# Reordering the opening of a two-layer attention kernel: exponentials of the gates behind copies of queries

## The chip, the cores and the metric

The kernel runs on one core of a Trainium2 chip. Its time is in device microseconds (us), from start to end of one execution; the span inside it runs from the first to the last profiled instruction. The engines are TensorE (PE, with its weight loads as PEld), VectorE (DVE), ScalarE (ACT), GpSimd (POOL) and SyncE (SP), which here only issues DMAs. Each engine works through its own queue in order and waits on semaphores for the others.

## The reference, cut to what matters

Two layers, each of an attention with a compressive memory (A) and a linear attention (B), over 2048 tokens of width 512 in 32 heads of 16.

```python
def _A_ref(x, wq, wk, wv, wo, beta):      # N = 4 segments of L = 512 tokens
    q, k, v = ...                         # x @ wq, x @ wk, x @ wv by head and segment
    phi = lambda t: jnp.where(t > 0, t + 1.0, jnp.exp(t))
    mask = (ar[:, None] < ar[None, :]) * -1e9
    g = sigmoid(beta).reshape(1, H, 1, 1) # one gate per head
    for s in range(N):
        p = softmax(qs @ ks.T * Dh ** -0.5 + mask)
        a_mem = (phi(qs) @ M) / (phi(qs) @ z + 1e-6)
        o = g * a_mem + (1.0 - g) * (p @ vs)
        M, z = M + phi(ks).T @ vs, z + phi(ks).sum()
    return o @ wo

x = A_x
for _ in range(2):
    x = x + _A_ref(layernorm(x), A_wq, A_wk, A_wv, A_wo, A_beta)
    x = x + _B_ref(layernorm(x), B_wqkv, B_w_phi, B_wo)
```

`_B_ref` projects to queries, keys and values, maps queries and keys through a small matrix per head and two softmaxes, and attends linearly.

## The kernel before, in words

The program is first written down as a list of 3416 numbered operations (`Program.add`), each with what it reads and writes and the engines that it may run on. Then `replay` deals them out by four tables that were written out beforehand: `ORDER` lists the operations in one sequence, from which every engine takes its own queue in that order (a number over 10000 is a matmul group that runs interleaved with the one before it, a negative one a filler of matmuls on zeros); `ENGINE` gives the engine of each operation that may run on several; `SLOTS` gives the buffer, or the bank of PSUM, of each tile when it is first used; and `AFTER` adds pairs (x, y) by which x waits for y although no data ask for it. `finalize` then writes every engine's queue with its semaphore waits.

```python
for n, x in enumerate(ORDER):
    if x < 0:
        f = self.idle_op((-1 - x) // 16, (-1 - x) % 16)
        ...
    op = ops[x % 10000]
    if len(op.eng) == 1:
        op.on = op.eng[0]
    op.need = set(op.deps)
    for t in list(op.pre) + op.tiles:
        if t.slot is None:
            k, p = int(next(slots), 36), t.pool
            ...                     # the tile waits for all users of the buffer's last holder
    self.queues[op.on].append(op.i)
for x, y in AFTER:
    ops[x].need.add(y)
```

The work is cut into segments of 512 tokens (for A) or chunks of 512 (for B) and tiles of 128 tokens. In the opening, `setup` loads four tiles of x, the weights of A and beta (`load`, L592; beta is the last of the six loads on ACT's queue), and then more loads on SP (`late_loads`), among them the raw key and query weights of B into two EQ buffers. `ln` normalizes the four tiles (statistics L806, L807; variance L816 and its power on POOL, L818; xn on DVE, L822) and TensorE transposes them (L606), with a copy to xA (L584). `a_proj` projects each tile: keys feature-major with three copies into K (L926 on ACT, L927 on DVE), scaled by the columns `even` 0 and 1 (L727), which keep one half of the heads; a shifted copy `lo` of xA (L912); a packed copy KP of K on POOL (L943); phi of the keys (exponential L834 on ACT, minimum L835 and sums L837 on DVE); queries with a copy into QT (L584); values with a copy into VT. The third and fourth tiles take their keys through `ktok` and a DMA transpose into K (L590).

The gates: exp(-beta) (L730) and exp(+beta) (L731) on ACT; from the second DVE makes the column `cb` = 1 + exp(beta) (L734), and copies it as the 17th column of each head into both VT buffers, four tiles each (L742, eight copies), so that the matmul of weights and values returns each head's sum divided by 1 - g. The first becomes g (L732, L733, L739), which scales the memory's state.

`a_att` computes scores in units of 1024 columns (L525), takes exponentials on ACT (L1109), masks the diagonal on DVE and POOL (L1115 with the pattern `modd`, L1118), multiplies by VT, divides (L1143, L1144) into O, and transposes O by DMA into OT for the output projection with WA_o. `fold_weights` turns the raw key and query weights of B, transposed by DMA from EQ into OT (four transposes, L590), into WB_k and WB_q.

Of the kernel before, what the change touches and what calls it, by code (L numbers as in the profile page):

```python
# [33 lines left out]
    0, 20, -401, 1, 2, 81, 4, 6, 8, 10, 3, 82, 5, 26, 7, 21, 24, 25, 9, 22, 11, 16, 53, 18, 54, 55, 60, 17, 56, 12, 61, 27, 62, 57, 63, 13, 35, 33,  # L34
    58, 64, 59, 67, 65, 84, 66, 68, 69, 85, 34, 74, 102, 70, 103, 86, 75, 104, 76, 71, 77, 115, 87, 105, 72, 83, 88, 89, 78, 106, 90, 73, 37, 91, 36,
    107, 116, 40, 45, 92, 96, 110, 46, 117, 47, 97, 38, 28, 48, 93, 29, 49, 157, 94, 98, 121, 50, 95, 30, 158, 209, 122, 346, 210, 123, 344, 31, 177,
    32, 347, 124, 133, 178, 212, 166, 10161, 345, 335, 125, 134, 348, 162, 349, 337, 79, 108, 51, 211, 127, 338, 426, 109, 336, 80, 167, 130, 128,
    339, 351, 340, 99, 350, 129, 131, 111, 352, 341, 118, 135, 342, 119, 168, 132, 112, 136, 343, 159, 1129, 179, 120, 214, 137, 160, 164, 163, 52,
    113, 138, 14, 169, 180, 100, 215, 114, 139, 145, 165, 146, 101, 1131, 140, 170, 182, 10193, 142, 143, 148, 181, 147, 183, 149, 144, 171, 172, 389,
    194, 173, 425, 187, 404, 126, 405, 150, 371, 185, 184, 174, 353, 188, 753, 198, 196, 406, 354, 746, 436, 199, 186, 355, 1138, 151, 195, 356, 200,  # L40
    15, 189, 1140, 197, 190, 359, 230, 152, 213, 380, 231, 191, 217, 232, 754, 192, 381, 755, 233, 201, 203, 368, 141, 216, 204, 382, 202, 175, 239,
    10234, 756, 744, 369, 240, 218, 176, 205, 206, 219, 220, 207, 235, 221, 222, 208, 757, 258, 223, 1141, 422, 224, 383, 39, 225, 263, 259, 43, 386,
    384, 1132, 370, 407, 387, 264, 423, 385, 427, 388, 242, 246, 10248, 438, 247, 424, 266, 362, 19, 260, 363, 236, 249, 439, 357, 153, 226, 758, 154,
    360, 364, 361, 244, 10250, 227, 365, 237, 228, 245, 446, 238, 372, 437, 229, 251, 241, 373, 252, 448, 243, 428, 374, 253, 1130, 447, 449, 366,
    268, 10270, 450, 375, 377, 429, 451, 254, 269, 367, 255, 440, -20, 453, 452, 271, 287, 378, 454, 261, 390, 256, 262, 1139, 288, 745, 430, 747,
    257, 272, 379, 1142, 441, 431, 282, 290, 273, 376, 391, 1143, 432, 392, 294, 283, 1133, 434, 433, 1134, 276, 393, 277, 395, 396, 289, 442, 435,
    295, 274, 1135, 464, 1136, 275, 465, 358, 1137, 1145, 475, 265, 291, 41, 467, 476, 443, 267, 466, 296, 10298, 42, 408, 297, 397, 278, 285, 284,
    279, 44, 299, 1144, 409, 280, 1146, 468, 483, 281, 477, 410, 292, 306, 478, 748, 398, 469, 411, 293, 286, 472, 470, 749, 473, 307, 414, 311, 474,
    479, 399, 413, 300, 312, 301, 308, 415, 316, 759, 302, 317, 760, 313, 320, 480, 416, 321, 750, 318, 751, 309, 417, 481, 319, 303, 400, 761, 310,
    322, 304, 484, 323, 1192, 314, 324, 315, 485, 752, 325, 482, 471, 571, 10566, 418, 326, 305, 567, 327, 1177, 412, 556, 328, 572, 329, 402, 330,  # L50
    587, 10582, 156, 155, 558, 401, 813, 574, 559, 419, 816, 831, 403, 583, 798, 394, 771, 569, 573, 772, 588, 420, 762, 814, 421, 557, 780, 562,
    10564, 590, 815, 773, 545, 565, 585, 561, 832, 331, 584, 546, 833, 547, 563, 586, 333, 332, 589, 774, 455, 619, 10614, 568, 777, 615, 334, 570,
    778, 456, 548, 457, 620, 575, 763, 549, 764, 591, 779, 603, 10641, 458, 765, 459, 550, 604, 592, 460, 593, 551, 795, 642, 461, 552, 462, 594, 595,
    622, 598, 463, 553, 768, 617, 646, 599, 616, 554, 618, 576, 577, 555, 766, 796, 647, 578, 600, 444, 621, 579, 797, 623, 445, 637, 639, 601, 638,
    1162, 624, 580, 625, 605, 626, 606, 486, 602, 581, 640, 487, 596, 775, 607, 597, 627, 608, 489, 628, 651, 769, 653, 776, 488, 609, 610, 770, 611,
    654, 807, 629, 490, 612, 497, 613, 652, 498, 631, 494, 630, 808, 500, 649, 632, 644, 499, 657, 10655, 491, 495, 658, 643, 505, 809, 506, 656, 492,
    645, 665, 811, 781, 501, 496, 666, 782, 659, 783, 660, 648, 502, 810, 670, 10679, 784, 650, 635, 503, 786, 493, 507, 680, 668, 633, 671, 636, 675,
    661, 812, 676, 662, 504, 836, 677, 667, 789, 678, 634, 785, 790, 834, 508, 669, 791, 663, 835, 837, 694, 10689, 787, 792, 838, 664, 510, 839, 509,
    695, 683, 672, 511, 684, 690, 840, 681, 841, 799, 788, 682, 842, 703, 673, 800, 674, 704, 699, 10701, 697, 801, 685, 700, 686, 793, 1147, 802,
    794, 512, 692, 687, 702, 825, 688, 691, 826, 513, 805, 804, 729, 10727, 693, 817, 728, 806, 696, 852, 818, 730, 698, 705, 819, 853, 706, 707, 820,  # L60
    823, 767, 708, 827, 855, 718, 10713, 854, 829, 709, 560, 710, 714, 856, 1163, 711, 1164, 712, 719, 863, 716, 857, 864, 822, 715, 1165, 723, 10725,
    1148, 724, 858, 717, 1149, 824, 860, 726, 720, 861, 721, 1150, 722, 731, 828, 862, 949, 10947, 1151, 803, 732, 948, 733, 734, 830, 950, 941, 735,
    736, 1159, 866, 942, 983, 10972, 865, 737, 930, 738, 984, 1168, 867, 931, 739, 871, 932, 973, 1160, 985, 1169, 868, 1166, 1161, 859, 951, 10988,
    821, 869, 1170, 872, 986, 975, 952, 1153, 873, 933, 974, 1154, 989, 742, 934, 976, 1155, 991, 990, 967, 10956, 743, 1171, 937, 740, 987, 968, 938,
    992, 845, 1178, 957, 1179, 969, 741, 935, 970, 846, 1180, 999, 843, 1004, 1000, 939, 1181, 971, 936, 1174, 1175, 844, 1172, 1005, 847, 977, 1173,
    978, 848, 993, 940, 994, 995, 1156, 979, 980, 850, 1026, 11042, 1176, 849, 996, 1157, 1198, 1027, 851, 1001, 1158, 1199, 1002, 997, 1189, 1043,
    953, 1007, 959, 1190, 1003, 1200, 998, 1024, 981, 1183, 1006, 1025, 982, 1184, 954, 958, 1008, 1009, 1201, 1010, 1185, 1022, 11031, 960, 874,
    1191, 1032, 875, 955, 1011, 1012, 876, 1034, 961, 962, 1013, 963, 877, 1014, 964, 870, 1033, 1023, 1040, 965, 878, 885, 966, 886, 1016, 1041, 882,
    1015, 888, 1028, 1036, 11038, 1017, 879, 887, 1204, 1167, 1037, 1205, 880, 889, 883, 1206, 1039, 1055, 11050, 1029, 893, 1187, 1030, 890, 1051,
    894, 1035, 1044, 891, 1045, 1056, 884, 1064, 1046, 1065, 1062, 1053, 1052, 895, 1047, 1020, 1063, 1048, 1186, 1049, 1066, 11060, 1021, 1018, 1054,  # L70
# [13 lines left out]
    1525, 923, 928, 1442, 1416, 1454, 1526, 1407, 1271, 1417, 1527, 1270, 1455, 1528, 924, 1418, 1459, 1426, 1272, 1287, 1428, 1460, 1529, 1288, 1433,  # L84
# [80 lines left out]
    3324, 3325, 3328, 3326, 3329, 3342, 3330, 3321, 3338, 3289, 3343, 3331, 3344, 3317, 3339, 3345, 3340, 3341, 3318, 3306, 3319, 3377, 3346, 3353,  # L165
    3378, 3380, 3354, 3355, 3356, 3357, 3381, 3335, 3358, 3359, 3360, 3387, 3336, 3361, 3383, 3388, 3389, 3332, 3390, 3384, 3385, 3337, 3386, 3307,
    3347, 3391, 3407, 3348, 3350, 3408, 3349, 3379, 3322, 3409, 3410, 3382, 3398, 3351, 3365, 3399, 3400, 3401, 3362, 3366, 3411, 3363, 3402, 3395,
    3333, 3364, 3412, 3403, 3334, 3392, 3396, 3404, 3393, 3413, 3394, 3405, 3367, 3397, 3414, 3406, 3352, 3415,
)
AFTER = (  # L170
    (21, 20), (23, 1246), (25, 82), (26, 82), (27, 60), (31, 346), (56, 55), (63, 60), (70, 34), (77, 76), (83, 67), (91, 78), (179, 112), (201, 754),
    (202, 141), (211, 345), (212, 346), (218, 216), (237, 361), (238, 227), (242, 385), (243, 227), (262, 378), (267, 1136), (286, 284), (289, 392),
    (290, 745), (291, 1145), (309, 750), (313, 415), (315, 1192), (339, 335), (340, 336), (349, 344), (407, 384), (450, 449), (451, 366), (468, 1144),
    (535, 1540), (570, 421), (574, 412), (575, 557), (584, 412), (589, 762), (590, 328), (602, 605), (617, 461), (645, 809), (648, 643), (667, 504),
# [1306 lines left out]
```

## Time and profile before

| | |
|---|---|
| Median of 3 runs | 470.28 us (469.51 to 471.39) |
| Profiled execution | 469.92 us |
| Its span | 468.2 us |
| Mean granted TensorE clock | 0.993 of full |
| Busy in the span: PE, DVE, ACT, POOL | 97%, 89%, 91%, 54% |
| Chain that ended last, by engine | PE 50%, ACT 33%, DVE 9%, DMA 3%, POOL 3% |

A row of the timeline gives start, length, engine, line, operation, what is written and read, and in brackets the idle time of the engine before it with what ended it. A row of the chain gives start, length and the engine with its tile. Rows of stretches give, for each engine, the busy time and the number of instructions, and then the clock that TensorE was granted. Ends of matmuls are modelled.

### The profile page before, as it was taken

To read this page: it belongs to the slowest core of one execution; us is meant where nothing else is said; L and a number is where in the kernel's file an instruction comes from. 1 tells how busy PE (TensorE), PEld (TensorE's weight loads), DVE (VectorE), ACT (ScalarE), POOL (GpSimd) and SP (SyncE) were. 2 spreads that over 40 slices of the span, in tenths; PEclk is the share of its full clock that TensorE was granted. 3 is DMA by queue.
4 is the path that set the end of the run, shared out by engine and by line. 5 is a ranking of instruction groups with operands and counts; after the bars stand their busy time and mean duration, and the time that the engine had idled before them with its cause. 6 is when DMAs were issued, how large, how long until landed. Compare 5 with 4: busy or idle time off the path is not lost.

```text
span 468.2 us, 18975 instructions
## 1 busy us (share of the span) xinstructions
PE 452.7 (97%) x8208; PEld 312.7 (67%) x8208; DVE 418.9 (89%) x1038; ACT 428.0 (91%) x665; POOL 251.0 (54%) x406
## 2 busy tenths in 40 slices
PE   7899999999999999999999999999999999999897
PEld 6686667677756556647778667777775756755653
DVE  6899999979998989788998999999999798988884
ACT  4899999999999999986999899999999999999633
POOL 3666646666755767520066372875686676741100
PEclk9899999999999989999999999999999999999999
DMA  8979742243211224120334346234341122631366
GB/s 266 199 172 170 104 71 48 48 70 69 48 26 26 48 46 64 31 57 14 69 76 86 70 63 100 48 70 76 67 67 25 25 47 50 92 48 24 69 132 183
DMA packets 115091, 35.85 MB, mean 77 GB/s; under 512 B 106816, under 2 KB 115008, under 8 KB 115008
## 3 DMA queue, kind: packets, MB, share of 16 engines
q1 hardware_dynamic: 112896, 32.80, 38.4%
q10 hardware_dynamic: 2112, 1.84, 1.2%
q8 instruction: 64, 1.05, 1.0%
q14 instruction: 19, 0.16, 0.1%
HBM read 6.32 MB, written 2.10 MB: 18 GB/s over the span
## 4 chain that ended last, share of the span: by engine, by line
PE 50%; ACT 33%; DVE 9%; DMA 3%; POOL 3%; issue 1%; ACTq 0%; POOLq 0%
PE PS L525 49%; ACT PT L1109 23%; ACT Ek L1205 3%; DMA beta<-in_A_beta_dram 2%; ACT EQ L1290 2%; POOL PT L1118 1%; DVE xn L822 1%; DVE Vt L1233 1%; DMA OT<-O 1%; POOL D L1115 1%; ACT QT L584 1%; ACT PT L1290 1%; ACT phi L964 1%; PE PS L606 1%; DVE D L1115 1%
## 5 line engine op out<-in xcount | busy, mean ns | idle before, releaser
L1109 ACT ACTIVATE PT<-PS 128x1024 bf16<-128x1024 f32 x288 | 282.0, 1062 | 5.8 <-PE PS L525 4.3
L1115 POOL TENSOR_TENSOR D<-PT,modd 128x256 bf16<-128x256 bf16 x118 | 80.7, 695 | 48.8 <-ACT PT L1109 21.1
L1118 POOL TENSOR_SCALAR_AFFINE_SELECT PT<-PT 128x512 bf16<-128x512 bf16 x128 | 82.6, 657 | 36.3 <-DVE D L1115 28.1
L525 PEld LDWEIGHTS PS<-VT,PT 128*128 128x128 bf16 x2048 | 74.4, 96 | 16.1 <-POOL PT L1118 1.9
L525 PE MATMUL PS<-VT,PT 128*128 128x17 bf16 x2048 | 81.0, 171 | 1.1 <-DVE O L1144 0.5
L525 PE MATMUL PS<-QT,K 32*128 32x64 bf16 (+2 forms) x2176 | 76.0, 214 | 2.4 <-ACT QT L584 1.7
L525 PE MATMUL PS<-VT,D 128*128 128x17 bf16 x512 | 59.5, 171 | 0.0
L525 PEld LDWEIGHTS PS<-QT,K 32*128 32x128 bf16 x2176 | 40.9, 93 | 20.3 <-ACT PT L1109 9.9
L1309 POOL COPY O<-rho 128x512 bf16<-128x512 bf16 x26 | 16.5, 656 | 52.0 <-DVE rho L1302 26.2
L525 PEld LDWEIGHTS PS<-VT,D 128*128 128x128 bf16 x512 | 43.2, 96 | 0.0
L1115 DVE TENSOR_TENSOR D<-PT,modd 128x256 bf16<-128x256 bf16 x138 | 40.4, 311 | 2.9 <-ACT PT L1109 1.6
L1212 POOL TENSOR_TENSOR Vt<-Ek 128x512 f32<-128x512 bf16 x24 | 28.0, 1167 | 24.1 <-ACT Ek L1205 18.9
L1233 DVE TENSOR_TENSOR Vt<-PS,Zk 128x1024 bf16<-128x1024 f32 (+1 forms) x34 | 38.9, 1154 | 0.4 <-PE PS L525 0.2
L806 DVE BATCH_NORM_STATS2 stats<-X 128x6 f32<-128x512 bf16 x56 | 37.5, 683 | 1.8 <-DMA X<-in_A_x_dram 1.4
L1205 ACT ACTIVATE Ek<-PS 128x512 bf16<-128x512 f32 x64 | 37.1, 653 | 1.8 <-PE PS L525 1.5
L1170 DVE TENSOR_TENSOR X<-X,PS 128x512 bf16<-128x512 bf16 x50 | 33.6, 680 | 3.2 <-PE PS L525 2.8
L525 PE MATMUL PS<-xA,WA_q 128*128 128x128 bf16 x512 | 36.0, 219 | 0.0
L525 PE MATMUL PS<-WA_k,xA 128*128 128x256 bf16 x256 | 35.7, 278 | 0.2
L525 PE MATMUL PS<-WA_v,xA 128*128 128x256 bf16 x256 | 35.5, 274 | 0.0
L525 PEld LDWEIGHTS PS<-xA,WA_q 128*128 128x128 bf16 x512 | 30.0, 98 | 4.4 <-issue 1.1
L525 PE MATMUL PS<-WB_o,OT 128*128 128x512 bf16 x128 | 32.2, 380 | 0.2 <-DMA OT<-O 0.2
L525 PE MATMUL PS<-WA_o,OT 128*128 128x512 bf16 x128 | 32.0, 380 | 0.4 <-DVE OT L584 0.2
(156 smaller groups left out, 938.7 us busy)
## 6 DMA issues: line engine op xcount, KB each, us to landing
X<-in_A_x_dram SPq DMA_DIRECT2D x3, 512.0 KB, 11.5
out_dram<-X SPq DMA_DIRECT2D x10, 128.0 KB, 1.9
EQ<-in_B_wqkv_dram SPq DMA_DIRECT2D x2, 512.0 KB, 5.6
out_dram<-X ACTq DMA_DIRECT2D x6, 128.0 KB, 2.4
OT<-O SPq DMA_TRANSPOSE x42, 3.2
WB_v<-in_B_wqkv_dram SPq DMA_DIRECT2D x1, 512.0 KB, 10.6
WA_o<-in_A_wo_dram SPq DMA_DIRECT2D x1, 512.0 KB, 3.9
WB_o<-in_B_wo_dram SPq DMA_DIRECT2D x1, 512.0 KB, 5.4
```

The lines of the kernel that those rows point to most:

```text
L525: return e.matmul(o, l, r, start=st, stop=sp, tile_position=(basep(l), basep(o)))
L584: emit = {"act": lambda e: e.activation(dst(), src(), ACT.Copy), "dve": lambda e: e.tensor_copy(dst(), src())}
L806: self.dve(lambda e, t=t, src=src: e.bn_stats(self.stats[:, t, :], src()), 0.603, [held() if held else R("X", t)], [R("stats", t)], name=" ...
L1109: self.act(lambda e, st=st, pt=pt: e.activation(pt.ap[:].rearrange("p b c -> p (b c)"), self.ps[:, st.slot[0] * 512:st.slot[0] * 512 + 102 ...
L1115: self.either(lambda e, d=d, k=k, pt=pt: e.tensor_tensor(d.ap[:, :, k, :].rearrange("p b (z c) -> p b z c", z=2), self.ends(pt.ap[:, :, 25 ...
L1118: self.pool(lambda e, q=quarters: e.affine_select(q(), q(), [[0, 4], [1, 128]], ALU.is_ge, 0.0, base=0, channel_multiplier=-1), 0.6, [pt() ...
L1170: self.dve(lambda e: e.tensor_tensor(X[:, t, :], X[:, t, :], self.bank(gen), ALU.add), 0.6, [R("X", t), gen()], [R("X", t)], name="resid")
L1205: self.act(lambda e, sgn=sgn, Ek=Ek, gen=gen: e.activation(Ek.ap[:, sgn, :], self.bank(gen), ACT.Exp, scale=1.0 - 2.0 * sgn), 512, [gen()] ...
L1212: self.pool(lambda e, Ek=Ek, sums=sums: e.tensor_tensor(sums(), *(Ek.ap[:].rearrange("p s (h j) -> p s h j", h=H)[:, :, :, 8 * k:8 * k + 8 ...
L1233: self.dve(lambda e, w=w, n=n, Vt=Vt, Zk=Zk, gen2=gen2: e.tensor_tensor(self.signed(Vt)[:, w, :, 0:16], self.bank(gen2).rearrange("p (h d) ...
L1290: self.act(lambda e, sgn=sgn, g=g, gen=gen: e.activation(E(sgn, g), self.bank(gen), ACT.Exp, scale=1.0 - 2.0 * sgn), 512, [gen()], [part(s ...
L1309: P.add(("act", "pool"), {"act": lambda e, dst=dst, src=src: e.activation(dst(), src(), ACT.Copy), "pool": lambda e, dst=dst, src=src: e.t ...
```

## The change

Only the four tables change. No operation is added or taken away. The first rows of `ORDER`, before and after:

```diff
 ORDER = (
-    0, 20, -401, 1, 2, 81, 4, 6, 8, 10, 3, 82, 5, 26, 7, 21, 24, 25, 9, 22, 11, 16, 53, 18, 54, 55, 60, 17, 56, 12, 61, 27, 62, 57, 63, 13, 35, 33,
-    58, 64, 59, 67, 65, 84, 66, 68, 69, 85, 34, 74, 102, 70, 103, 86, 75, 104, 76, 71, 77, 115, 87, 105, 72, 83, 88, 89, 78, 106, 90, 73, 37, 91, 36,
-    107, 116, 40, 45, 92, 96, 110, 46, 117, 47, 97, 38, 28, 48, 93, 29, 49, 157, 94, 98, 121, 50, 95, 30, 158, 209, 122, 346, 210, 123, 344, 31, 177,
...
+    22, 20, -401, 0, 1, 26, 81, 27, 3, 2, 82, 5, 4, 7, 6, 9, 8, 11, 10, 53, 16, 18, 54, 55, 60, 56, 17, 21, 61, 24, 62, 57, 25, 63, 58, 33, 59, 28,
+    64, 12, 67, 65, 84, 66, 74, 85, 68, 103, 75, 69, 86, 70, 104, 83, 102, 89, 71, 29, 90, 34, 76, 87, 105, 30, 115, 77, 88, 72, 106, 116, 92, 91, 73,
+    96, 107, 121, 97, 78, 110, 37, 117, 40, 45, 31, 98, 93, 46, 36, 47, 177, 94, 157, 346, 178, 209, 122, 95, 210, 48, 344, 123, 133, 49, 124, 32,
...
 AFTER = (
-    (21, 20), (23, 1246), (25, 82), (26, 82), (27, 60), (31, 346), (56, 55), (63, 60), (70, 34), (77, 76), (83, 67), (91, 78), (179, 112), (201, 754),
+    (23, 1246), (24, 60), (25, 62), (28, 33), (29, 74), (32, 344), (70, 75), (83, 68), (91, 71), (179, 112), (201, 754), (202, 141), (211, 344),
...
```

Read as queues of the engines, this is what changes:

| Engine | Order before | Order after |
|---|---|---|
| ACT | `lo` of tile 2; K copies 1a, 1b, 1c, 2b; exp(+beta); exp(-beta); K copy 2c; phi's exponential, tile 1; copies of queries, tiles 2 and 1; score exponentials 158, 210, 178 | K copies 1b, 1c; phi's exponential, tile 1; K copy 2c; exp(+beta); copies of queries, tiles 2 and 1; exp(-beta); score exponentials 178, 210, 158 |
| DVE | H8b, `even` 0, xn 2, statistics 3, `even` 1, statistics 4, xn 3, K copy 2a, xn 4, copy of xA 3, `cb`, VT columns among phi and statistics | `even` 0, xn 2, statistics 3 and 4, K copy 1a, `lo` of tile 2, xn 3, `even` 1, K copies 2a and 2b, copy of xA 3, `lo` of tile 3, xn 4, `cb`, VT columns, most of them later; H8b far later |
| PE | ... second tile's keys; queries 2 (first half); transpose 3; first tile's keys by head; queries 2, 1; scores 157, 209; third tile's keys; scores 177 | ... second tile's keys; first tile's keys by head; queries 2 (first half); transpose 3; queries 2, 1; scores 177, 157, 209; third tile's keys |
| POOL | `ident` and H8, power 1, ..., powers, `lo` 1, KP 1, KP 2, pieces of `modd`, `lo` 3 | `ident`, power 1, H8, power 2, pieces of `modd` among powers, `lo` 1, KP 1, KP 2 |
| SP | raw keys' load; transpose of K (tile 3); transpose of raw keys, first half; two transposes of xn; raw queries' load; transpose of K (tile 4); transpose of raw queries, first half; WA_o's load | transpose of K (tile 3); two transposes of xn; transpose of K (tile 4); raw keys' load; raw queries' load; transpose of raw queries, first half; transpose of raw keys, first half; WA_o's load |

(1a is the copy into K of the first tile that uses `even` 0; b and c are the two with `even` 1.) Behind the first 26 groups of PE, the first 27 of ACT, 22 of POOL and 18 of SP, and behind the first 68 of DVE (in the new count) save for H8b's cast, the queues are the same as before. The copies 1a and 2b and the `lo` copies of tiles 2 and 3 change engine (from ACT, ACT, ACT and POOL to DVE) in `ENGINE`. `SLOTS` deals the ten PT buffers and some others out in another rotation, so that tiles take turns with other tiles than before; the numbers of buffers are the same.

More of the change, by code (lines that the diff above doesn't have):

```diff
@@ L198 @@
 SLOTS = (
-    "10000204510210000310282090141131530052001212101030211400221133071110002302225001411216020123123210011117003511002829051043010104022504312005"
-    "40121090015402200014832234701023002543000421312501300315701034111200110511000381902011022111421110514052300005231703000216001110300102031112"
-    "20119081112100227003120303023002140120510112130716022140010200113012201211334315061203012100021317010351403133121311000332270611200340010200"
-    "00210050811313020191102301203120310202100914010301132001400308205022132253360232020150712112111601090224432805131123233701632509300322151221"
-    "04083034100302261932300230433113110010300240532035720201480526110011240003300022111322370222152410133042133410000809210320221511013201016031"
-    "00020403110021920010070222381010150311110042025376970010318250161123123103410220000413003223064331053203210302101007006722170135301620127261"
+    "00211311215020403010020704304105010022100401113180231023136051101000231122390114122101013211232300612115003911002428051043000107032504312005"
+    "60721080150402300114432234001020002553600421312007312035901030111300110511400301702011032110421300514022300005251903000218061110300103031112"
+    "21117001112100229005110303023003140120210112130419022180610210115012201311332318091203014130021316010021503133121811000332260910201320510220"
+    "00210040113313020131002301207180310202100512000301132301400107205022832253340932021100612112141501070224832905132143230601032507300322151241"
+    "08093034000302221732300230133113411010350240536035820201400922110011210003350022411326380222152410133002133410000107210320221419013221015031"
+    "00020003110061820010070222311010140391110022025375870010314210161123123103410220000413003223064331053203210302101007006722170135301620127261"
     "20175012102006401331317302020010827007621101600600523117002020280933204131003051101001070031211100120030226190321100041283113023102101302023"
@@ L210 @@
     "02133290151002102601350072073251252200021821403100112233000121511171101289640150346030120030010434112112151003521700211002210320322020312311"
-    "0233020076122306111204500160763027341"
+    "0233020076223106111204500160763027341"
 )
```

2 lines of the change are left out of this document (1 added, 1 removed), and 114 rows, old and new, of tables (AFTER, ORDER).

## The prediction

> **What bounds the kernel now.** I read the page's head, then the chain of work that ended last in the first 60 us, the timeline of the opening, the busy time by stretch, and the DMA issues with their landings.
>
> ```profile
> span 468.2 us, 18975 instructions
> PE 452.7 (97%) x8208; PEld 312.7 (67%) x8208; DVE 418.9 (89%) x1038; ACT 428.0 (91%) x665; POOL 251.0 (54%) x406
> ```
>
> Three engines are nearly full over the span. No engine's order changes past the opening but for one small cast, so only the opening can move. The chain there (start, length, what):
>
> ```profile
> 3.27 8.73 DMA beta<-in_A_beta_dram
> 12.00 0.02 issue
> 12.03 0.23 ACT rd L731
> 12.25 0.12 ACT rd L730
> 12.37 0.36 ACT K L926
> 12.73 0.49 ACT phi L834
> 13.22 0.98 ACT QT L584 x2
> ```
>
> Beta lands at 12.00. Between it and the two copies of queries stand two exponentials, a copy into K and an exponential of keys; the copies end at 14.20 and the score units follow. The idle gaps around it (in brackets, with what ended them):
>
> ```profile
> 10.56 1.50 PE L525 MATMUL PS<-xA,WA_q 128*128 128x128 bf16 x24
> 12.03 0.23 ACT L731 ACTIVATE rd<-beta 128x32 f32<-128x32 bf16 x1 [1.54 <-DMA beta<-in_A_beta_dram]
> 12.29 0.18 DVE L734 TENSOR_SCALAR cb<-rd 128x32 bf16<-128x32 f32 x1 [1.66 <-ACT rd L731]
> 13.76 0.39 PE L525 MATMUL PS<-QT,K 32*128 32x128 bf16 x8 [1.70 <-ACT QT L584]
> 16.71 0.69 DVE L584 CAST ktok<-PS 128x512 bf16<-128x512 f32 x1 [0.49 <-PE PS L525]
> 17.26 2.17 ACT L1109 ACTIVATE PT<-PS 128x1024 bf16<-128x1024 f32 x2 [1.12 <-PE PS L525]
> 19.13 0.42 DVE L584 COPY xA<-PS 128x512 bf16<-128x512 bf16 x1 [0.18 <-PE PS L606]
> ```
>
> ACT, DVE and PE each lose over 1.5 us around beta; after that only small gaps are left. By stretch (length; busy time and count of PE, PEld, DVE, ACT, POOL; granted clock; DMA share; GB/s):
>
> ```profile
> 4.00:7.41 3.41, 2.06 (x25) 1.57 (x23) 2.94 (x11) 1.84 (x3) 1.52 (x3) 1.00 1.07 362
> 10.83:14.24 3.41, 1.63 (x31) 1.29 (x28) 1.84 (x9) 2.21 (x7) 1.51 (x5) 1.00 1.12 363
> 14.24:17.65 3.41, 3.40 (x39) 2.22 (x40) 2.92 (x9) 2.29 (x3) 2.00 (x6) 0.50 0.68 205
> 20.00:30.00 10.00, 10.00 (x193) 8.89 (x191) 10.00 (x29) 10.00 (x16) 6.20 (x10) 1.00 1.06 170
> ```
>
> TensorE's clock was halved from 14.24 to 17.65, right after a stretch in which it was busy 1.63 of 3.41 us. From 20 to 30 PE, DVE and ACT are all full: what the opening saves reaches the end only as far as the slowest of the three passes it on.
>
> **The change, part by part.**
>
> *ACT.* Its order becomes: two copies into K of the first tile (both need the second `even` column), the key exponential, one more copy into K, exp(+beta), the two query copies, exp(-beta), the score exponentials. So only exp(-beta) goes behind the queries; exp(+beta) still waits until 12.00 in front of them. Two copies into K and a `lo` copy leave ACT for DVE. There the second `even` slides behind more work:
>
> ```profile
> 7.82 0.15 DVE L727 TENSOR_REDUCE even<-H 128x1 f32<-128x4 f32 x1
> 7.88 0.68 DVE L806 BATCH_NORM_STATS2 stats<-X 128x6 f32<-128x512 bf16 x1
> 8.33 2.15 ACT L926 ACTIVATE K<-PS,even 128x512 bf16<-128x512 f32 x4
> 8.60 0.18 DVE L807 BATCH_NORM_AGGREGATE mv<-stats 128x2 f32<-128x6 f32 x1
> 8.90 0.41 DVE L822 TENSOR_SCALAR xn<-X,mv,rstd 128x512 bf16<-128x512 bf16 x1
> 9.23 0.74 DVE L927 TENSOR_SCALAR K<-PS,even 128x512 bf16<-128x512 f32 x1
> 14.08 0.41 DVE L837 SCALAR_TENSOR_TENSOR PhiK<-PS,phi 128x256 bf16<-128x256 f32 x1
> 21.70 0.22 DVE L912 COPY xA<-xA 128x256 bf16<-128x256 bf16 x1
> ```
>
> 7.82 plus 0.68 and 0.18 (statistics), 0.74 (a K copy moved here), 0.22 (`lo`) and 0.41 (xn) puts it at 10.05, and about 9.95 since neighbours overlap a little. ACT then needs some 0.5 + 0.5 (four K copies took 2.15), 0.49 and 0.36 (the chain's rows), 1.85 us: done at about 11.9, which the wait for beta covers with 0.1 to spare; without that cover each us late is a us on the queries. The query copies start behind one exponential, at about 12.2 instead of 13.22, and end at 13.25 instead of 14.20: of the chain's terms 0.12, 0.36 and 0.49 go, 0.97 us.
>
> *PE.* The first tile's two key groups move ahead of the queries; the second waits for its `lo` copy. I put the end of the queries at 12.4 (12.06 now), still ahead of their copies. Then a score unit that needs both copies goes first, at about 13.30, where today the first unit starts at 13.76 and waits again for the second copy until 14.20. The score exponentials start at 13.75 instead of 14.20, 0.45 us; three units then stand in a row, so ACT's 1.12 gap goes too. ACT could gain 0.45 + 1.12 = 1.57.
>
> *The clock.* PE's idle in the stretch 10.83 to 14.24 shrinks from 1.78 to about 0.9 us, busy 74%, above the 60% (2.06 of 3.41) after which the clock stayed whole. I take it as whole. The price, from rows:
>
> ```profile
> 14.79 1.89 PE L525 MATMUL PS<-WA_k,xA 128*128 128x256 bf16 x8
> 22.66 1.05 PE L525 MATMUL PS<-WA_k,xA 128*128 128x256 bf16 x8
> ```
>
> 0.84 us for these eight alone, an estimated 1.4 for the 3.41 us. With the earlier start PE could gain up to 0.9 + 1.4 = 2.3. [...]
>
> *DVE.* Added before 12.29: the two K copies (0.74, and near 0.41 for the half-size one) and two `lo` copies (0.22 each), 1.59 us. Its idle 1.66 covers them, and H8b's cast leaves that stretch. The gate column `cb` still waits for exp(+beta), so the next work begins at 12.29 as now, and from there on it is the same work in another order: DVE can save only its gaps, 0.49 + 0.18 = 0.67.
>
> ```profile
> L742 DVE COPY VT<-cb x8: 220/242/705, 12.5 to 22.6; 128x32 bf16<-128x32 bf16 x8
> 26.19 0.23 PE L525 MATMUL PS<-VT,PT 128*128 128x17 bf16 x3
> ```
>
> VT's eight columns (median 0.24) slide back among DVE's work. Their reader stands at 26.19 and the last column now ends at 23.3: 2.9 us of cover, and 0.24 a column if that were gone.
>
> *New waits.* A key group on PE now needs a phi buffer that DVE frees at about 15.1, against 14.7 when PE could take it: 0.4 of PE idle, with the other key, value and score groups queued behind it. The first tile's values wait, as now, for DVE's xA copy (19.13), which gets more DVE work ahead: up to 1 us of PE idle. Both take from PE's 2.3, not from what it has today. POOL gets the mask's pieces and the powers in another order; busy for 54% of the span, it has room.
>
> *Buffers.* The ten PT buffers, and a few others, are dealt out in another rotation through the whole kernel, so a score unit waits for other earlier readers. By the trace's times each of these had ended when its buffer is taken again, give or take 0.07, so I put nothing. What PE waits for PT in all, over the span, is this row of its waits:
>
> ```profile
> PE PS L525 <- ACT PT L1109: 0.2, 1, 0.2
> ```
>
> Were such a wait to come up in each half of the kernel, it would cost some tenths.
>
> *SP.* The raw keys' load moves behind four transposes, next to the raw queries' load; behind those comes the raw queries' transpose, which holds SP until they land.
>
> ```profile
> 18.82 1.33 SPq L590 DMA_TRANSPOSE OT<-EQ  x1
> 24.03 0.58 SPq L592 DMA_DIRECT2D EQ<-in_B_wqkv_dram  x1
> 28.39 1.86 SPq L590 DMA_TRANSPOSE OT<-EQ  x1
> 35.55 1.23 SPq L590 DMA_TRANSPOSE OT<-O  x1
> EQ<-in_B_wqkv_dram SPq DMA_DIRECT2D x1, 512.0 KB, 6.8
> EQ<-in_B_wqkv_dram SPq DMA_DIRECT2D x1, 512.0 KB, 4.3
> 39.04 0.38 PE L525 MATMUL PS<-WA_o,OT 128*128 128x512 bf16 x1
> ```
>
> The raw queries would be issued near 26.4 (24.03 now) and land 4.3 to 6.8 later, 30.7 to 33.2. Behind them stand 1.86 + 1.33 + 0.58 = 3.77 of issues, so SP is free for the first attention output's transpose between 34.5 and 37.0. That output would be ready near 34.85 (35.55 less the gain). I take the lower end, no cost, since 4.3 was measured in this part of the kernel and 6.8 in the crowd of first loads.
>
> *Sum.* ACT 1.57, PE at most 2.3, DVE 0.67, and SP from 0 to a loss of 1.45 (35.55 to 37.0) at the bottom. I take 0.7, DVE's, because from 20 to 30 DVE is as full as the others and hands them their inputs. The profiled execution took 469.92 us (span 468.2 and 1.7 around it): 469.92 - 0.7 = 469.2. It stands 0.36 below the median of the three runs, so in medians 470.28 - 0.7 = **469.6 us**.
>
> **Rivals.**
> 1. *DVE does not hold it back.* What PE and ACT need goes first on DVE, VT's columns and the gate's arithmetic go last; ACT's whole 1.57 passes: 470.28 - 1.6 = 468.7. For it: DVE is 89% busy over the span and can catch up later. Against: the full stretch from 20 to 30.
> 2. *Slower: SP is late.* If the raw queries land 6.8 us after their issue, the output's transpose is issued at 37.0 instead of 35.55. PE takes its result in order at 39.04, 3.5 after the present issue, so it resumes at 40.5 at the latest and, with some slack, 1.2 later than today; everything queued on PE waits with it: 470.28 + 1.2 = 471.5. It begins to cost when they land past 31.1 (34.85 - 3.77) and turns the change into a loss past about 32. For it: two loads of 512 KB back to back behind a transpose. [...]
> 3. *It does not do what it says.* The second `even` comes 0.5 late or more, the copies of queries move little, the clock still halves: 0.2 is left, 470.1. For it: ACT's margin of 0.1 before 12.00. Against: DVE's 1.66 of idle for the extra work.
>
> **How the numbers follow.** Forecast 0.52; rival 1 0.22; rival 2 0.15; rival 3 0.11. Half a per cent is 2.35 us, about what a measurement of this kernel can tell from no change. No case reaches it alone; with the runs' scatter (469.51 to 471.39) part of rival 1 ends below 467.9 and part of rival 2 above 472.6: faster 0.10, same 0.82, slower 0.08. The range runs from rival 1 less 0.7 of scatter to rival 2: 468.0 to 471.5.
>
> **What would show it.** First score matmul near 13.3; PE's gap before it under 1.1; clock 1.00 from 14 to 18; no gap of ACT near 17; `cb` still at 12.3 and DVE full from there to 30 without the 0.49 and 0.18; the first output's transpose issued before 35.0. It is wrong if PE waits at the first output projection, if the half clock is still there, or if the span moves by more than 2 us either way.

## The result, and the profile after

| | Kernel before | Changed kernel |
|---|---|---|
| Median | 470.36 us (469.51 to 471.39, 4 runs) | 474.59 us (474.16 to 475.48, 4 runs) |
| Profiled execution, its span | 469.92, 468.2 | 474.83, 473.1 |
| Mean granted TensorE clock there | 0.993 | 0.993 |

The ratio is 1.0091, with a 95% interval of 1.0066 to 1.0117: slower by 4.2 us, where a gain of 0.7 was forecast. A second measurement (below) gave 1.0068 (1.0039 to 1.0098). The medians here and below are over all executions, the ratios leave out those in a disturbed state, among them the first profile of experiment 4, at a mean clock of 0.555.

Of the changed kernel, first the chain of work that ended last (start, length, what):

```profile
36.76 0.68 DVE VT L584 x2
37.44 4.72 DMA OT<-O
42.16 0.05 issue
42.21 7.28 PE PS L525 x64
```

A DMA now stands in it: the transpose of the first attention output, on which the first output projection waits. The timeline of SP's issues, and of TensorE at that place:

```profile
25.76 1.17 SPq L592 DMA_DIRECT2D EQ<-in_B_wqkv_dram  x2
33.08 3.69 SPq L590 DMA_TRANSPOSE OT<-EQ  x2
36.81 0.58 SPq L592 DMA_DIRECT2D WA_o<-in_A_wo_dram  x1
37.44 1.26 SPq L590 DMA_TRANSPOSE OT<-O  x1
...
38.36 0.40 PE L525 MATMUL PS<-VT,PhiK 128*128 128x136 bf16 x4
42.21 1.04 PE L525 MATMUL PS<-WA_o,OT 128*128 128x512 bf16 x2 [3.45 <-DMA OT<-O]
```

SP issues the two raw loads at 25.76 and then nothing until 33.08: its next entry, the transpose of the raw queries, waits for their landing at 33.06. WA_o's load and the output's transpose come behind both raw transposes. The output's transpose goes out at 37.44 (35.55 before), and TensorE resumes at 42.21 (39.04 before) after 3.45 us without work. Its DMA rows in that stretch (median us to landing last):

```profile
EQ<-in_B_wqkv_dram SPq DMA_DIRECT2D x2, 512.0 KB, 6.3
WA_o<-in_A_wo_dram SPq DMA_DIRECT2D x1, 512.0 KB, 4.2
OT<-O SPq DMA_TRANSPOSE x1, 4.7
```

The stretches of 3.41 us (length; PE, PEld, DVE, ACT, POOL busy; clock; DMA share; GB/s), from 10.83, from 14.24, then the one that holds the stall and the two after it:

```profile
10.83:14.24 3.41, 2.62 (x40) 2.40 (x40) 3.31 (x11) 2.97 (x8) 2.84 (x7) 1.00 1.07 337
14.24:17.65 3.41, 3.05 (x57) 2.53 (x58) 3.38 (x13) 3.03 (x6) 0.86 (x2) 1.00 0.24 63
38.10:41.51 3.41, 0.66 (x12) 0.48 (x9) 1.62 (x5) 2.25 (x4) 2.04 (x4) 1.00 0.99 237
41.51:44.92 3.41, 2.71 (x13) 0.70 (x14) 0.75 (x2) 0.24 (x1) 0.02 (x1) 0.50 1.11 238
44.92:48.34 3.42, 3.42 (x25) 2.04 (x24) 2.41 (x7) 1.83 (x3) 2.00 (x4) 0.50 0.81 109
```

The half clock of 14.24 is gone, as forecast (though not by this change, see below), but two half-clock stretches follow the stall.

Matching TensorE's matmul groups one by one between the two traces gives the account in time. At 38.36 the changed kernel leads by 0.44. The first output projection starts 3.17 late, a swing of 3.6. Through the two half-clock stretches this grows to 5.95 and holds at 6.1 until 165 us; there the old trace has its second half-clock stretch (167.84 to 171.25) and the new one has none, and at the end 4.9 is left, the difference of the spans.

In the opening:

```profile
13.04 0.23 ACT L731 ACTIVATE rd<-beta 128x32 f32<-128x32 bf16 x1
13.18 1.12 ACT L584 ACTIVATE QT<-PS 128x512 bf16<-128x512 f32 x2
14.20 0.22 ACT L730 ACTIVATE rd<-beta 128x32 f32<-128x32 bf16 x1
14.80 2.85 ACT L1109 ACTIVATE PT<-PS 128x1024 bf16<-128x1024 f32 x3 [0.38 <-PE PS L525]
```

Beta landed 1.0 later in this execution (13.02 instead of 12.00), but behind it the queue does what was forecast: the copies follow one exponential, the first score exponential comes 1.78 behind beta's landing instead of 2.20, and three of them run without the old gap of 1.12.

### The profile page after: what moved, and what is told of

The parts are those of the page before. It is cut to its first block, busy times and chain, and to the rows that moved or that the text cites. A ratio compares the mean times of both kernels' runs of the same rounds, so it can differ in the third digit from the quotient of the medians.

```text
span 473.1 us, 18972 instructions
## 1 busy us (share of the span) xinstructions
PE 453.3 (96%) x8208; PEld 312.3 (66%) x8208; DVE 419.8 (89%) x1042; ACT 426.8 (90%) x662; POOL 250.9 (53%) x405
## 4 chain that ended last, share of the span: by engine, by line
PE 48%; ACT 36%; DVE 10%; DMA 2%; issue 1%; POOL 1%; ACTq 0%; POOLq 0%
PE PS L525 47%; ACT PT L1109 25%; ACT Ek L1205 3%; ACT EQ L1290 2%; DMA X<-in_A_x_dram 1%; DVE stats L806 1%; DMA OT<-O 1%; DVE xn L822 1%; ACT K L1290 1%; ACT PT L1290 1%; PE PS L606 1%; DVE Vt L1233 1%; ACT phi L964 1%; DVE O L1347 1%; POOL PT L1118 1%
## 5 line engine op out<-in xcount | busy, mean ns | idle before, releaser
L525 PE MATMUL PS<-WA_o,OT 128*128 128x512 bf16 x128 | 33.6, 395 | 4.0 <-DMA OT<-O 3.4
```

Of the source, the lines that this page charges most:

```text
L525: return e.matmul(o, l, r, start=st, stop=sp, tile_position=(basep(l), basep(o)))
```

## The experiments

Numbers in the diffs are those of `ORDER`: 12 wphi's load, 13 and 14 the loads of the raw keys and raw queries, 426 and 436 the transposes of their first halves, 125 and 140 the transposes of K, 352 and 343 those of xn, 15 WA_o's load, 225 the transpose of the first attention output, 226 the first output projection. Ratios are to the kernel before, on the same chip.

**1. SP's queue put back.**

```diff
 SP, changed kernel
-12, 125, 352, 343, 140, 13, 14, 436, 426, 15, 225, 427
+12, 13, 125, 426, 352, 343, 14, 140, 436, 15, 225, 427
```

> The changed kernel with SP's queue alone in its old order: raw key load behind wphi, its transpose behind the transpose of tile 3's K, raw query load ahead of the other three transposes. All compute queues and buffers stay those of the changed kernel. Theory Q (SP's queue carries the loss: the transpose of the raw query load holds SP until the load has landed at 33.06, so the first attention output's transpose is issued at 37.44 and lands at 42.16, TensorE stalls 3.4 us before the first output projection, and two half-clock windows after the stall cost 2.8 more): no wait before the first output projection, full clock from 40 to 50 us, and the opening's lead of 0.45 to 0.8 us kept: 469.0 to 470.3 us. Theory O (the loss stems from the engines' new order in the opening, where `cb` and the first exponentials came later than the forecast had them): about 474.6, as the changed kernel. Theory S (the buffers dealt in another order): also 474.6.

Measured: 470.87, ratio 0.9988 (0.9959 to 1.0017), by the ratio 0.6 us less than the kernel before. The issues on SP and the projection:

```profile
32.04 0.58 SPq L592 DMA_DIRECT2D WA_o<-in_A_wo_dram  x1
34.75 1.23 SPq L590 DMA_TRANSPOSE OT<-O  x1
38.25 1.03 PE L525 MATMUL PS<-WA_o,OT 128*128 128x512 bf16 x4
```

No wait stands in front of the projection, which starts 0.79 earlier than before. The whole loss is gone while every compute queue and every buffer stays as changed, so theories O and S fall.

**2. SP's new queue alone, in the kernel before** (the same diff, the other way round).

> The kernel before with SP's queue alone in its new order; every compute queue and all buffers stay the old ones. Theory Q: the first output projection waits for its transposed input until about 42.2, and the stall and its half-clock windows cost 5.5 to 6.5 us with no lead from the opening to set against them; against that, about 1.0 us if the half-clock window at 168 us goes, as it did in the changed kernel: 474.5 to 476.5 us. Theories O and S: 470.4, as before.

Measured: 475.51, ratio 1.0107 (1.0062 to 1.0152). The timeline of TensorE there:

```profile
41.19 1.85 PE L525 MATMUL PS<-WA_o,OT 128*128 128x512 bf16 x4 [2.26 <-DMA OT<-O]
```

The same wait, with the old opening. SP's queue is enough for the loss, and by experiment 1 nothing else is needed.

**3. Only the raw keys' load put back.**

```diff
 SP, changed kernel
-12, 125, 352, 343, 140, 13, 14, 436, 426, 15, 225
+12, 13, 125, 352, 343, 140, 14, 436, 426, 15, 225
```

> The changed kernel with one load moved back: the raw key load stands behind wphi again, everything else on SP (both raw transposes behind the raw query load, and WA_o's load behind them) as changed. Theory Q in its narrow form (the two loads back to back make the raw queries land 6.7 us after their issue, where the load alone took 4.3): the raw queries land near 30, SP is free near 34, the first attention output's transpose is issued when its input is ready (about 35), no stall: 469.0 to 470.3. If instead the order of the two raw transposes and WA_o's load behind them is enough (a wide form of Q: any wait of SP for the raw queries at that place): some of the stall stays, 471 to 474. Theories O and S: 474.6.

Measured: 471.53, ratio 0.9999 (0.9971 to 1.0027), 0.001 above experiment 1.

```profile
33.55 0.73 SPq L592 DMA_DIRECT2D WA_o<-in_A_wo_dram  x1
34.58 1.40 SPq L590 DMA_TRANSPOSE OT<-O  x1
39.12 1.04 PE L525 MATMUL PS<-WA_o,OT 128*128 128x512 bf16 x4 [0.87 <-DMA OT<-O]
```

Issued without delay, the output's transpose still left a wait of 0.87: it landed 4.49 after its issue, with WA_o's load, issued 1 us ahead of it, in flight until 38.10. In experiment 1 that load had landed 1.9 after the transpose's issue and the transpose took 3.40. So the stall has two parts: SP held by the raw queries' transpose, and WA_o's load pushed next to the output's transpose. Each of the first two expectations holds in part: the transpose was issued as soon as its input was ready, as in the narrow form, but some of the stall stayed, as in the wide one. And the raw queries' load took 5.63 us here with the other load long landed, not the 4.3 of the narrow form.

**4. The raw keys' transpose behind the output's.**

```diff
 SP, changed kernel
-13, 14, 436, 426, 15, 225, 427
+13, 14, 436, 15, 225, 426, 427
```

> The changed kernel with the transpose of the raw keys' half moved on SP from ahead of WA_o's load and the first attention output's transpose to behind them; both raw loads stay late and back to back, and the transpose of the raw queries' half still waits for them. Theory Q: the raw queries' transpose holds SP until about 35.3, WA_o's load follows at 35.4 and the attention output's transpose at about 36.0 in place of 37.44, landing beside WA_o's load at 40.4 to 41.0; TensorE waits 1.6 to 2.3 us in place of 3.4, followed by one half-clock window or none: 471.3 to 473.3 us. Theories O and S: 474.6.

Measured: 473.04, ratio 1.0053 (1.0022 to 1.0085), as expected. The trace is that of another execution:

> The same kernel as the one with the raw keys' transpose behind the first attention output's transpose, for a profile only: the profile taken of it had a granted clock of 0.555 throughout and can't be read beside the others. Theory Q as there: the attention output's transpose issued near 36.0, landing at 40.4 to 41.0, a wait of TensorE of 1.6 to 2.3 us.

Measured: 473.78, one execution. TensorE:

```profile
38.64 1.04 PE L525 MATMUL PS<-WA_o,OT 128*128 128x512 bf16 x4 [1.04 <-DMA OT<-O]
...
48.66 0.29 DVE L943 COPY KP<-K 128x512 bf16<-128x512 bf16 x1 [2.05 <-DMA K<-ktok]
...
50.21 0.40 PE L525 MATMUL PS<-O,OT 128*128 128x128 bf16 x4 [1.41 <-DVE WB_k L584]
```

The output's transpose went out at 34.21 already (the loads were early in this execution), the wait is 1.04 in place of 3.45 and no half clock follows (1.00 granted from 39.40 to 42.80): a smaller dose, a smaller stall, below the 1.6 to 2.3 expected. At 50.21 a further 1.41 is lost: a weight fold waits for a copy on DVE, and DVE had stood 2.05 until a transpose of K landed at 48.64. That transpose was issued at 43.78 (43.38 in the kernel before) and took 4.86 (3.41 before), with a packet of an instruction fetch in flight from 46.37 to 47.64, of which experiment 5 has more. That the moved transpose of the raw keys causes this second wait is not shown.

**5. The stall filled with work.** 32 matmuls on constant data before 226.

```diff
 ORDER, changed kernel
-226
+-519, 226
```

> The changed kernel with 32 extra matmuls on constant data (about 3.3 us at full clock, by the 25 of the start, which are 0.10 us apart there) in front of the first output projection, so that TensorE works through the stall; their results are never read. If the half clock from 41 to 48 us follows from the stall's idleness: the stall's 3.4 us stays, the two half-clock windows and their 2.8 us go: 471.3 to 472.3 us. If the half clock has another cause (a fixed time, the mix of the work): 474.6. If the matmuls themselves delay the projection: over 475.

Measured: 480.64, ratio 1.0207 (1.0170 to 1.0244): 5 to 6 us slower than the changed kernel, against the first two expectations; the third, a delay by the filler itself, isn't it either, since the projection started at 41.37, just behind the landing of its input at 41.32. Yet the clock did what the first one said, in the stretch with the stall and the next one:

```profile
37.94:41.35 3.41, 3.40 (x35) 2.99 (x31) 0.93 (x3) 1.26 (x3) 1.05 (x2) 1.00 1.20 175
41.35:44.76 3.41, 3.39 (x38) 1.96 (x39) 2.25 (x4) 1.99 (x3) 1.48 (x3) 1.00 1.12 247
```

The loss came later, in steps of 0.3 to 1.3 between 80 and 457 us; at about half of them TensorE itself waits for a DMA transpose, at most others for DVE. I counted the transposes after 50 us that took over 3.95 us from issue to landing: 14 in the kernel before, 16 in the changed one, 26 here. Every one of them, in every trace, had a packet of an instruction fetch in flight, or one within 0.3 us before its issue (30 of the 60 under 3.3 us in the kernel before had one too). The output's transpose in the changed kernel and in experiment 2 is no such case: no packet was near it. New theory: 64 more instructions (matmul and weight load) on TensorE shift all its later fetches, and more of them fall on transposes.

**6. The same filling, with whole fetch packets.** The filler is made 60 columns wide instead of 240 in the matmul that it emits, and 128 of them are put in.

```diff
-226
+-2055, 226
```

> The changed kernel with the stall filled a second time, now by 128 narrow matmuls (60 columns) in place of 32 wide ones (240 columns): again about 3.4 us of work on constant data ahead of the first output projection, results never read. With its weight load each matmul is two instructions, so TensorE's queue grows by 256 instructions and not by 64; the traces show TensorE's instructions fetched in packets of 16384 bytes, about one for each 256 instructions. Theory F (the 32 wide matmuls moved every later fetch against the DMA transposes, which then took 4.4 us where they took 3.1): with one whole packet more the later fetches meet the same transposes as in the changed kernel, 14 to 18 transposes after 50 us take over 3.95 us (26 in the first filled kernel), and only the half clock's 2.8 us go: 471.3 to 472.5 us on the scale where the changed kernel has 474.6. If the filling itself costs the time: 479 to 481 again. If the half clock doesn't follow from the idle stall: 474.6.

Measured: profiled execution 471.78, its trace with 16 slow transposes and no half clock before the last 0.2 us:

```profile
37.94:41.35 3.41, 3.41 (x116) 3.41 (x114) 1.78 (x6) 2.41 (x4) 2.20 (x4) 1.00 1.59 269
41.35:44.76 3.41, 3.41 (x55) 2.02 (x52) 1.54 (x3) 1.25 (x2) 0.82 (x2) 1.00 0.99 214
```

Group by group its trace runs with that of the changed kernel up to the projection (3.08 late against 3.17) and then stays at 3.0 where the other goes to 5.95. So the two half-clock stretches cost 2.8 us in the changed kernel's profile (from 3.17 to 5.95), and by these traces they follow from the idle stall: the three that leave it idle (the changed kernel twice, experiment 2) have them, the two that fill it have none.

The median says less: 474.91, ratio 1.0065 (1.0032 to 1.0098), not below the changed kernel. Two things in the record bear on that. The filler is too long: in this trace the projection's input landed at 40.95, and the filler ran until the projection started at 42.12, so up to 1.2 us of the delay is its own. And the other eleven executions had a mean clock of 0.985 to 0.993, by my estimate two to four half-clock stretches somewhere (one of 3.41 us at 0.50 in a span of 470 us lowers the mean by 0.0036), as the kernel before has them. The mean clocks put the stretches that the stall adds at 0.6 a run in the changed kernel's second measurement (0.9899, against 0.9922 in the kernel before) and at 1.2 in experiment 2 (0.9870 against 0.9914), and those of the filled kernel at none (0.9902 against 0.9903). That is less than the traces show, so how much of the 2.8 us is in the average stays open.

**7. The fetch shifted, nothing else.** 32 narrow matmuls behind the warming ones of the start.

```diff
 ORDER, kernel before
-0, 20, -401, 1, 2
+0, 20, -401, -513, 1, 2
```

> The kernel before with 32 narrow matmuls (60 columns, constant data, results never read) behind the 25 warming ones of the start, in TensorE's free time between 5.20 and 6.07 us: no order, no wait and no transfer is touched, but every later instruction of TensorE stands 64 places further back. Theory F (where the instruction fetch falls on a DMA transpose, the transpose takes 1.2 to 1.9 us longer, and the queues are tuned round the places where it falls now): the number of transposes over 3.95 us after 50 us rises from 14 to over 20, and the time to 473 to 479 us. If fetches don't matter: 470 to 471.4, as before.

Measured: 476.69, ratio 1.0133 (1.0081 to 1.0185), 23 slow transposes. The fillers made the first transposes start at 6.77 instead of 6.07, so at most 0.7 of the 6.3 us is theirs. An example, from 74 to 83 us, the fetch packets and the landings in the kernel before and then in this one:

```profile
q8 instruction: 1, 0.02, 0.8%
EQ<-xn SPq DMA_TRANSPOSE x1, 3.2
K<-ktok SPq DMA_TRANSPOSE x1, 3.3
```

```profile
q8 instruction: 1, 0.02, 0.7%
EQ<-xn SPq DMA_TRANSPOSE x1, 4.5
K<-ktok SPq DMA_TRANSPOSE x1, 4.1
```

Here the packet, from 77.19 to 78.14, fell on both transposes in mid-flight (75.05 to 79.55 and 76.32 to 80.38); in the kernel before it began at 80.19, when the first had landed and the second had 0.5 us to go. Theory F's forecasts hold, and experiment 5's trace loses time at the same places as this one (near 80, 101, 107, 326 and 346 us here, 3 to 4 us later there), though the two have different queues on SP and different openings. So the shift of 64 instructions, which they have in common, is the likely cause of experiment 5's loss. Why some transposes with a packet near them are slow and others are not stays open.

**8. More use of TensorE ahead of the remaining half clock**, on top of experiment 1.

```diff
-1344
+-70, 1344
...
-2665
+-35, 2665
```

> The changed kernel with SP's old queue order, plus six matmuls (240 columns, constant data, results never read) on TensorE in two places that precede the half-clock windows left in that kernel's trace: four into the 0.47 us gap at 164.05, two ahead of the score unit at 349.18. If those windows follow from low use of TensorE in the 3.41 us ahead of them: no half clock at 166 and 350 us, and 1.3 and 0.8 us less than with the old queue order alone: 468.3 to 469.5 us where that has 470.9. If not, or if the six matmuls (0.6 us) stand in the way: 470.5 to 471.5.

Measured: 471.80, ratio 1.0009 (0.9977 to 1.0041): no gain. The half clock came earlier, and lasted three stretches:

```profile
160.42:163.83 3.41, 3.00 (x102) 2.48 (x100) 3.12 (x12) 3.41 (x7) 2.08 (x6) 1.00 0.02 5
163.83:167.24 3.41, 3.41 (x79) 3.01 (x79) 1.85 (x6) 2.82 (x4) 2.53 (x6) 0.50 0.42 82
```

The four matmuls ran at 163.69, held for 0.41 by the exponential whose bank of PSUM they use, so the deciding stretch was all but over: the trial says nothing on whether fuller use would have kept the clock. At 350 there was no half clock, as expected, but the stretches fell otherwise here and one trace doesn't tell why. The six matmuls also bring 12 instructions, and 20 transposes after 50 us took over 3.95 us here, where experiment 1 had 16: a cost of that kind can stand against a gain. What the rows show is that TensorE's records have it busy 3.00 of 3.41 in the deciding stretch: busy time alone does not foretell this half clock, and what does stays open.

**9. The changed kernel again.**

> The changed kernel itself a second time, for a second profile and a closer ratio beside the experiments. Theory Q: the first attention output's transpose is issued after 36.0 behind the two raw transposes and lands near 41 to 42.2 beside WA_o's load; TensorE waits 2.4 to 3.6 us at the first output projection and one or two half-clock windows of 3.41 us follow at once; 1.007 to 1.012 of the kernel before. If stall or half clock were an accident of the one profile: another place or none, and under 1.005.

Measured: 473.80, ratio 1.0068 (1.0039 to 1.0098), at the lower end of what was expected.

```profile
35.89 1.25 SPq L590 DMA_TRANSPOSE OT<-O  x1
40.74 1.89 PE L525 MATMUL PS<-WA_o,OT 128*128 128x512 bf16 x4 [3.00 <-DMA OT<-O]
```

```profile
37.16:40.57 3.41, 0.58 (x11) 0.40 (x8) 1.54 (x5) 2.17 (x4) 1.97 (x3) 1.00 1.07 269
40.57:43.98 3.41, 3.24 (x15) 0.90 (x16) 1.28 (x2) 0.77 (x1) 0.55 (x1) 0.50 1.38 222
```

The same stall, this time with one half-clock stretch behind it.

**10. Beta's load early, in the kernel before.**

```diff
 ACT's loads
-0, 2, 4, 6, 8, 10
+0, 2, 4, 10, 6, 8
```

> The kernel before with beta's load (8 KB) issued ahead of the loads of WA_q and WA_v on the queue that ScalarE issues, nothing else moved. It tests what bounds the opening. If beta's landing does (12.0 to 13.0 in the kernel before and the changed one, with the first exponential of a score unit 2.20 us behind it in the old order and 1.73 to 1.78 in the new one): beta lands before 10, its two exponentials are done before the copies of queries, and the first exponential of a score unit comes 1.0 to 1.2 us behind the first copy of queries, at 13.2 to 13.9 in place of 14.2 to 14.7; 469.3 to 470.2 us where the kernel before has 470.4. If the loads of the x tiles and weights bound it just as closely: the first exponential stays at 14.2 to 14.7 and so does the time.

Measured: 473.02, ratio 1.0043 (1.0016 to 1.0071). Beta landed at 8.89 and its exponentials were out of the way, but the chain of this kernel begins with another load:

```profile
2.75 7.80 DMA WA_q<-in_A_wq_dram
10.55 0.05 issue
10.60 0.62 PE PS L525 x8
```

The first score exponential stayed at 14.18. WA_q's load had landed at 8.33 before. The second expectation holds for the exponential: with beta out of the way, WA_q's load, itself issued 0.5 later for it, bounds the opening as closely as beta did. It does not hold for the time. Why the median rose by 2 us isn't settled; the profiled execution (469.01) doesn't show it.

**11. SP's old queue again, for the opening's size.**

> The changed kernel with SP's old queue order a second time, for the size of the opening's own gain, which the first comparison left between a gain of 1.9 us and a loss of 0.8. If the new opening saves 0.3 to 1.1 us (ScalarE's part of 0.45, seen behind beta in the traces, and more where no half-clock window falls): 469.3 to 470.1 us where the kernel before has 470.4, and the two comparisons together lie under 1. If it saves nothing: 470.4.

Measured: 470.38, ratio 0.9984 (0.9951 to 1.0017). With experiment 1 that is 0.6 and 0.75 us, and each interval includes none. Compared at equal mean clock, with the runs of all chips taken together: at 0.992 to 0.993 the kernel before took 471.1 (16 runs), the new opening with SP's old queue 470.2 (5), the changed kernel 473.8 (6); at 0.989 it was 471.3 (24), 470.9 (12) and 473.6 (2). Of the kernels run, this one has the lowest ratio, by about 0.1%, which is not clear of the noise.

## Why the prediction was wrong, step by step

*The step that failed* is SP: "I take the lower end, no cost, since 4.3 was measured in this part of the kernel and 6.8 in the crowd of first loads." Four quantities of it, measured in the changed kernel (two executions) and in experiment 2:

| | Forecast | Changed | Again | Exp. 2 |
|---|---|---|---|---|
| raw queries, issue to landing | 4.3 (up to 6.8) | 6.68 | 6.40 | 6.07 |
| from the raw queries' transpose to the output's | 3.77 | 4.36 | 4.11 | 3.49 |
| output's transpose issued at | 34.85 (up to 37.0) | 37.44 | 35.89 | 36.26 |
| its issue to the projection's start | 3.5 | 4.77 | 4.85 | 4.93 |

The landing came out at the upper end, which two loads of 512 KB issued 0.6 apart should have made the likelier one; in the six traces of the old queue, where the two loads are apart, it took 4.32 to 5.74, and 5.63 in experiment 3. So the pairing explains a part of the excess over 4.3, and the lower end was too low even for loads that stand apart. The last row was forecast by no case: the old 3.5 belongs to a transpose issued at 35.55, when WA_o's load had landed at 34.22, but the step that made SP late also put that load 0.63 ahead of this transpose. The moved step's neighbours count too: what stood behind the waiting entry was issued in one burst, both raw transposes, WA_o's load and the output's transpose between 33.08 and 38.70.

*Rival 2* had the mechanism and the place, and the point from which it decides (past 31.1). Its 1.2 was the mis-sized term: TensorE stood still for 2.3 to 3.5 and resumed 1.7 to 3.2 later than 39.04, since the landing behind WA_o's load added about 1.4. It then lost a further 1.5 to 2.8 in a trace to the half clock that no case had; how much of that is in the average over runs is open (experiment 6). What the traces show of one transfer behind another on SP's queue is this. WA_o's load landed 3.4 to 3.8 after the transpose's issue in the changed kernel twice and in experiments 2, 3, 4 and 6, and in all six the transpose landed 1.0 to 1.15 behind the load, 4.4 to 4.9 after its issue; in experiment 1, where the load landed after 1.9, it took 3.40. (In experiment 5 it took 6.14, with a fetch packet in flight too.) For the rival's condition, the two raw loads back to back, the difference is smaller: 6.07 to 6.68 so, 5.74 and 5.63 apart in experiments 1 and 3. That the order on the queue makes the later transfer wait is not shown by itself: no run moves one of them to another queue.

*ACT, the 0.97 and 0.45*: right only where beta lands last. With beta at 12.0 or later the first score exponential came 2.20 behind it in both traces of the old order, and 1.78, 1.73 and 1.72 in the three of the new one. With beta at 10.5 to 11.4 it was 2.6 to 3.0 behind it in the new order (three traces) and 2.27 in the old one (experiment 7): there ACT's own work, done at 11.8 to 12.4, bounds the new order, and nothing is gained. The margin of 0.1 ahead of beta was not there in the changed kernel's first profile either. The second `even` column came at 11.06 (about 10 forecast; 10.71 and 10.04 in experiments 1 and 9), ACT stood idle for 3.09 waiting for it, and its work was done at 13.07, with beta landed at 13.02. The condition of *rival 3*, `even` 0.5 late or more, was met; that beta was 1.0 late too, and hid the cost, was luck.

*The gap of 1.12 and DVE's cover*: right in that profile. `cb` started 0.29 behind beta (0.28 before), so the added copies cost nothing there; where beta landed at 10.5 to 11.4 it started 1.1 to 1.6 behind.

*The clock*: the half clock at 14.24 went, but not by this change: it was absent from the three other traces with the old order too (experiments 2, 7 and 10). Nor does a busy share above 60% keep the clock: TensorE was busy for 2.96 of 3.41 ahead of 167.84 in the kernel before, and for 3.36 ahead of 350.40 in experiment 1, and half clock followed both times. Half-clock stretches behind the same stall began at 41.52 and 40.57 in the changed kernel and at 41.27 in experiment 2, and each lasted 3.41 or 6.83. That one is absent from an execution, as the one at 14.24 is here, is by itself no gain of the change.

*The sum of 0.7*: near, 0.6 and 0.75 us where SP's queue is left alone, though neither interval excludes zero. That DVE sets this size was not tested, and the traces point elsewhere. Just ahead of the projection, matched group by group against the first profile, the new opening leads by 1.31 and the old one by 0.27 with beta at 12.49 and 12.54 (experiments 11 and 2), but by 1.46 and 1.50 with beta at 11.18 and 10.94 (9 and 7). On these four traces the opening gains about 1 us where beta lands late and nothing where it lands early, so the nearness of an average to 0.7 may be luck.

*New waits and buffers*: the phi wait was 0.24 (0.4 forecast), and the rotation of buffers costs nothing that shows, since experiment 1 keeps it.

## What to carry to other kernels

When a DMA is moved on an in-order queue (SP's, in the changed kernel, issued nothing between the two raw loads at 25.76 and the transpose at 33.08), walk the queue to the first entry behind it that feeds the bound engine, and price both ends of the wait: when that entry goes out, and what is in flight beside it when it does. Two large loads back to back should be priced at the crowded landing time (6.1 to 6.7 us here), and a transpose behind a load by the load's landing (it landed 1.0 to 1.15 behind it here). A lever that adds instructions to a long unrolled queue can also move its instruction fetches (with 64 more on TensorE a packet came at 77.19 in place of 80.19, and the time was 6.3 us longer), so a comparison of kernels with a few dozen instructions more need not be a clean one.

## What the runs showed of the hardware that was not expected

The instruction queue q8 has 64 packets of 16384 bytes in the kernel before and in the changed one, for TensorE's 16416 recorded matmuls and weight loads, about 256 each, and 65 in experiments 5, 6 and 7, which add instructions to TensorE alone. After 50 us no transpose without a fetch packet near it (of q8, or one of the 19 of q14) took over 3.44 us in any trace, and those with one took up to 5.5, though many of them no longer than 3.3. 64 extra instructions near the start went with 23 slow transposes in place of 14 and 6.3 us (experiment 7), 256 extra ones left the slow transposes at 16 (experiment 6).

A stretch of 3.41 us with TensorE busy 0.58 or 0.66 us was followed by half clock, but so were some with 2.96 to 3.36 us busy by their records. A stall of 1.04 or 0.87 was followed by none.
